# The unread elementwise result of a row maximum: one SBUF tile, or the PSUM bank it came from

## The chip, the cores and the metric

The kernel runs on one core of a Trainium2 chip. The metric is the device time of one execution in microseconds (us). The kernel before takes 852.42 us (median of 3 runs, 850.45 to 852.44).

The engines of the core have their own instruction queues, each worked in order, and wait for each other through semaphores: PE multiplies matrices and writes into PSUM, DVE (the vector engine) and ACT (the activation engine) read PSUM and SBUF, POOL works in SBUF, and SP issues the DMAs.

## The reference

One transformer block on 2048 tokens of width 512: layer norm, windowed causal attention with 32 heads of 16 columns and a window of 256 keys, output projection and residual, then a second layer norm and a gated MLP of hidden width 1376 with its residual.

```python
qkv = (x @ wqkv).reshape(B, S, 3, H, Dh)
scores = einsum("bhqd,bhkd->bhqk", q, k) * Dh ** -0.5
mask = (i - j >= 0) & (i - j < 256)
p = softmax(where(mask, scores, -1e9))
o = einsum("bhqk,bhkd->bhqd", p, v)
h = x + o @ wo
h2 = h + (sigmoid(ln(h) @ w_gate) * (ln(h) @ w_up)) @ w_down
```

The softmax needs, for each query and head, the maximum of the masked scores, or a number that serves as one. The change is in the place where that maximum is found.

## The kernel before, in words

Numbers are split into a high and a low float16 part, so a product of two matrices is three matmuls (`mm3`). The tokens go through attention in 8 blocks `b` of 256, and the heads in 8 groups `g` of 4. For a block and a group the stages are:

- `do_ln`, `do_qk`, `do_v`: layer norm, then the projections. PE writes into PSUM tiles of the ring `mm` (two banks), ACT and DVE copy them out in a high and a low part. SP moves queries and keys through DMAs into the tiles `SQ` and `SK`.
- `do_s`: the row maximum. For one head and one set of 64 query places, PE multiplies queries against 320 keys (at most two matmuls, L735, high parts alone) into a PSUM tile of the ring `s`, which has three banks. Then `row_max` lets DVE add the mask and take the maximum along the 320 columns in one instruction (L720). There are 512 of these, in the text called reductions, 448 of them 320 columns wide and the rest, of the first block, narrower.
- `do_m`: the maxima of a half of the heads are split, transposed by a DMA and written as extra rows into `SQ`, so that the next product comes out with the maximum subtracted.
- `do_st`: the scores once more, transposed and with both parts (`stp`, L789 to L800, ring of two banks). ACT takes the exponential (L765), POOL cuts the triangles at the window's ends off (L773, L778).
- `do_pv`, `do_o`, `do_wo`: probabilities times values (`pvp`, L826), transposed by DMA, divided by the row sums, multiplied by `wo` and added to `x`.

In the same stretch of time DVE, ACT and POOL also split and scale the weights of the MLP. The MLP (`do_ln2`, `do_pair`, `do_down`) follows the attention, with the last steps of attention in between.

An instruction of L720 has two results. The one that is read is the maximum, a column of the small tile `mq`; in the trace it appears as an instruction of its own, DVE_READ_ACCUMULATOR2_ANT, behind the CUSTOM_DVE_ANT_0 that does the work. The elementwise sum of scores and mask is also written, and nothing reads it: it goes to `junk`, a bfloat16 tile of 320 columns of which there is one (`bufs=1`).

The order of all instructions on every engine is written out: the table `ORDER` says which step of which piece comes next, and `Planner.run` follows it. The costs in the code have no part in it any more. What is not written by hand is the waits. The tile layer looks at what each instruction reads and writes, and gives it a wait on a semaphore wherever another instruction has to be done before. An instruction carries one wait itself; each further one stands as an EVENT_SEMAPHORE in front of it in the queue.

Of the kernel before, what the change touches and what calls it, by code (L numbers as in the profile page):

```python
# [28 lines left out]
BF16 = mybir.dt.bfloat16  # L29
# [6 lines left out]
P = 128  # L36
# [296 lines left out]
def tile_block(ctx, tc, x, wqkv, wo, wg, wu, wd, out):  # L333
    nc = tc.nc
    V, S, G, PE = nc.vector, nc.scalar, nc.gpsimd, nc.tensor
# [35 lines left out]
    def psum_tile(ring, shape, dt=F32):  # L371
        return psum.tile(shape, dt, name=ring + "p", tag=ring, bufs=RINGS[ring])
# [54 lines left out]
    swork = right.enter_context(tc.tile_pool(name="swork", bufs=2, side="right", reuse_waits="tile"))  # L427
# [16 lines left out]
    mask = swork.tile([P, 320], BF16, name="mask", bufs=1)  # L444
# [262 lines left out]
    def do_s(b, g, prio):  # L707

        p, hf = g // 2, g // 4
        needs = [("queries", b, p), ("filled", 0)] + [("keys", a, hf) for a in (b, b - 1) if a >= 0]  # L710
        left = 8

        def row_max(ps, c0, x, i, e, n):
            nonlocal left
            e, = yield {DVE_: (320 - c0) / 960 + 0.077}, [e]
            plan.free("s", n, e)
            junk = swork.tile([P, 320], BF16, name="junk", bufs=1)
            if (b, hf) not in mq:
                mq[b, hf] = swork.tile([P, 8, 4], F32, name="mq", bufs=4)
            V.tensor_tensor_reduce(out=junk[:, c0:], in0=ps[:, c0:], in1=mask[:, c0:], scale=1.0, scalar=-3.0e38,  # L720
                                   op0=ALU.add, op1=ALU.max, accum_out=mq[b, hf][:, x, i:i + 1])
            left -= 1
            if left == 0:
                plan.mark(("s", b, g), e)

        for jj in range(2):
            j = 2 * (g % 2) + jj
            for i in range(4):
                c0 = 0 if b else 256 - 64 * i
                e, n = yield {PE_: (320 - c0) / 2400 + 0.006}, needs, ["s"], 0.75  # L730
                ps = psum_tile("s", [P, 320])
                q = SQ[b % 2][0:96, 4 * p + j, i].rearrange("p u t -> p (u t)")
                for a, k0, k1, col in ((b - 1, 64 * i, 256, 0), (b, 0, 64 * i + 64, 256 - 64 * i)):
                    if a >= 0:
                        PE.matmul(ps[:, col:col + k1 - k0], q, SK[0:96, (2 * a + hf) % 5, 4 * (p % 2) + j, k0:k1], start=True, stop=True)  # L735
                plan.add(prio + (4 * jj + i) / 8, row_max(ps, c0, 4 * (p % 2) + j, i, e, n))
# [745 lines left out]
```

## Time and profile before

| what | before |
|---|---|
| median of 3 runs | 852.42 us |
| the profiled execution | 851.43 us |
| its span, first to last instruction | 849.6 us |
| mean granted TensorE clock | 0.97 of full speed |
| busy: PE, DVE, ACT, POOL | 90%, 85%, 52%, 33% of the span |
| first and last reduction (L720) | 45.4 and 482.7 us |

The profile has one row per group of instructions: line, engine, operation, out<-in with the sizes, how often, then the busy time and the mean of one, and behind a second bar the idle time of the engine just before them with what ended it. "DVE mq L720" as a releaser means that an engine waited until a reduction had written its maximum. "DVEq" is the sequencer of DVE, where the EVENT_SEMAPHORE instructions run. Matmuls are pipelined, and the records of successive ones overlap, so the busy share of PE is not the share of its peak.

### The profile page before, as it was taken

The page shows a single profiled execution, that of the slowest core. Times are in us where ns is not written, and L with a number is a line of the kernel's source. Part 1 is how long each engine was busy: PE and PEld are TensorE (multiplying, and loading weights), DVE is VectorE, ACT ScalarE, POOL GpSimd, SP SyncE. Part 2 cuts the span into 40 slices and gives each one's busy share as a digit, 9 for nine tenths or more (in the row PEclk, how much of TensorE's full clock was granted, in tenths as well). Part 3 has the DMA queues.
Part 4 walks back from the last instruction along what each step waited for, and adds up shares of the span by engine and source line. Part 5 has one row for each costly group of instructions (what it writes and reads, how often), then busy time and mean ns, then how long its engine had stood idle before and what let it go on. Part 6 is the DMA issues. An engine that isn't in the chain of part 4 may idle for free.

```text
span 849.6 us, 19062 instructions
## 1 busy us (share of the span) xinstructions
PE 765.7 (90%) x7014; PEld 509.9 (60%) x7014; DVE 725.9 (85%) x2052; ACT 438.2 (52%) x771; POOL 277.9 (33%) x342
## 2 busy tenths in 40 slices
PE   4788889999898899898999999658999999999997
PEld 3475557667666567566665555234756657567466
DVE  8988878888888889888987756999999888898983
ACT  5663656766568777767765766654221222112210
POOL 2632333424335354454445545655000000000000
PEclk9999988999999999999988999979999999999999
DMA  9585353374357459554965764974656458365536
GB/s 320 177 236 143 104 135 97 69 175 95 72 152 186 100 130 217 160 136 103 241 169 129 158 120 110 286 164 110 117 107 131 78 97 171 76 117 79 99 69 172
DMA packets 213326, 119.10 MB, mean 140 GB/s; under 512 B 176688, under 2 KB 185904, under 8 KB 213232
## 3 DMA queue, kind: packets, MB, share of 16 engines
q1 hardware_dynamic: 213232, 117.88, 59.1%
q8 instruction: 55, 0.90, 0.5%
q14 instruction: 39, 0.32, 0.1%
HBM read 43.65 MB, written 19.40 MB: 74 GB/s over the span
## 4 chain that ended last, share of the span: by engine, by line
PE 51%; DVE 32%; issue 7%; DMA 6%; ACT 1%; POOL 1%; DVEq 1%; SPq 0%; ACTq 0%; POOLq 0%
DVE junk L720 17%; PE sp L1131 12%; PE mmp L402 9%; PE mmp L1308 8%; PE pvp L826 6%; PE stp L1131 5%; PE sp L735 4%; PE pvp L1131 2%; PE stp L800 2%; PE stp L790 1%; DVE WD L951 1%; DMA x<-hl 1%; DVE sq L656 1%; PE mmp L1314 1%; DVE W L1021 1%
## 5 line engine op out<-in xcount | busy, mean ns | idle before, releaser
L720 DVE CUSTOM_DVE_ANT_0 junk<-sp,mask 128x320 bf16<-128x320 f32 (+4 forms) x512 | 239.5, 468 | 56.5 <-PE sp L735 9.3
L765 ACT ACTIVATE pa<-stp,kappa 128x512 f32<-128x512 f32 (+1 forms) x256 | 158.5, 645 | 81.5 <-PE stp L791 77.9
L735 PE MATMUL sp<-SK,SQ 96*128 96x256 f16 (+3 forms) x960 | 146.5, 237 | 37.3 <-DVE mq L720 29.1
L1131 PEld LDWEIGHTS <-x 128*128 128x128 f16 x1008 | 98.6, 98 | 105.9 <-issue 19.1
L1131 PE MATMUL sp<-W,x 128*128 128x512 f16 (+1 forms) x612 | 135.1, 361 | 14.2 <-DVE SQ L1154 10.5
L735 PEld LDWEIGHTS <-SQ 96*128 96x128 f16 x960 | 86.9, 99 | 86.9 <-issue 63.9
L402 PE MATMUL mmp<-xT,W 128*128 128x256 f16 x768 | 112.1, 276 | 4.9 <-DVE xT L357 2.2
L765 ACT ACTIVATE pb<-stp,kappa 128x512 f32<-128x512 f32 x128 | 85.6, 685 | 39.0 <-PE stp L800 38.1
L773 POOL TENSOR_SCALAR_AFFINE_SELECT pa<-pa 128x1024 f32<-128x1024 f32 x56 | 63.4, 1134 | 71.0 <-ACT pa L765 65.7
L402 PEld LDWEIGHTS <-W 128*128 128x128 f16 x768 | 70.3, 98 | 19.4 <-issue 5.0
L778 POOL TENSOR_SCALAR_AFFINE_SELECT pb<-pb 128x512 f32<-128x512 f32 x64 | 42.7, 667 | 71.4 <-ACT pb L765 64.2
L778 POOL TENSOR_SCALAR_AFFINE_SELECT pa<-pa 128x512 f32<-128x512 f32 x64 | 43.3, 677 | 65.3 <-ACT pa L765 65.3
L826 PE MATMUL pvp<-pa,VT 128*17 128x128 f32 (+1 forms) x1408 | 63.8, 312 | 0.6 <-DVE RH L838 0.6
L558 POOL TENSOR_TENSOR rs<-rs,nhalf 128x1 f32<-128x1 f32 x32 | 19.7, 619 | 131.5 <-DVE rs L555 131.2
L790 PE MATMUL stp<-SQ,SK 100*128 100x256 f16 x224 | 61.3, 278 | 0.0
L402 PE MATMUL mmp<-WO,oT 128*128 128x512 f16 x192 | 54.5, 405 | 5.5 <-DMA oT<-whl 5.3
L1131 PE MATMUL stp<-W,x 128*128 128x512 f16 (+1 forms) x264 | 58.2, 357 | 0.9 <-DVE SQ L359 0.6
L791 PE MATMUL stp<-SQ,SK 100*128 100x128 f16 x256 | 57.0, 223 | 0.2
L362 DVE TENSOR_TENSOR hr<-SQ,hr 128x512 f16<-128x512 f32 (+3 forms) x90 | 52.0, 588 | 2.4 <-ACT hr L355 1.6
L826 PEld LDWEIGHTS pvp<-pa,VT 128*17 128x17 f32 x1408 | 38.5, 99 | 24.7 <-issue 6.0
L800 PE MATMUL stp<-SQ,SK 100*128 100x256 f16 x256 | 50.5, 283 | 2.2 <-ACT pa L765 2.2
L1197 ACT ACTIVATE SQ<-sp,cg 128x512 f32<-128x512 f32 (+1 forms) x22 | 14.0, 638 | 73.2 <-PE sp L1131 73.2
(210 smaller groups left out, 1418.0 us busy)
## 6 DMA issues: line engine op xcount, KB each, us to landing
SQ<-sq SPq DMA_DIRECT2D x96, 128.0 KB
wr<-chunk SPq DMA_DIRECT2D x28, 256.0 KB
W<-wr SPq DMA_DIRECT2D x14, 512.0 KB
SK<-mem SPq DMA_DIRECT2D x16, 384.0 KB
chunk<-in_wd_dram SPq DMA_DIRECT2D x20, 256.0 KB
X<-in_x_dram SPq DMA_DIRECT2D x16, 256.0 KB
mem<-sk SPq DMA_DIRECT2D x8, 512.0 KB
out_dram<-X SPq DMA_DIRECT2D x16, 256.0 KB
```

The source lines that it names most:

```text
L402: PE.matmul(ps, a_of(a, k), b_of(b, k), start=(k == 0 and i == 0), stop=(k == n - 1 and i == 2))
L720: V.tensor_tensor_reduce(out=junk[:, c0:], in0=ps[:, c0:], in1=mask[:, c0:], scale=1.0, scalar=-3.0e38, op0=ALU.add, op1=ALU.max, accum_ou ...
L735: PE.matmul(ps[:, col:col + k1 - k0], q, SK[0:96, (2 * a + hf) % 5, 4 * (p % 2) + j, k0:k1], start=True, stop=True)
L765: S.activation(dst, a, AF.Exp, scale=kappa)
L773: G.affine_select(out=f, in_=f, pattern=[[0, 8], [-1, 128]], compare_op=ALU.is_gt, fill=0.0, base=0, channel_multiplier=1)
L778: G.affine_select(out=p, in_=p, pattern=[[0, 4], [1, 128]], compare_op=ALU.is_ge, fill=0.0, base=0, channel_multiplier=-1)
L790: PE.matmul(a[:, 128:384], ks(k0 + 1, g, j), qs(b, g, j, 0, 256), start=True, stop=True)
L791: PE.matmul(a[:, 384:512], ks(k0 + 3, g, j), qs(b, g, j, 128, 256), start=True, stop=True)
L800: PE.matmul(a[:, u, :], ks(k0 + 2, g, j + u), qs(b, g, j + u, 0, 256), start=True, stop=True)
L826: PE.matmul(ps[32 * j:32 * j + 17, u, q0:q1], VT[:, kt % 6, 8 * j + g, :], w[:, j, c:c + q1 - q0], start=first, stop=last, skip_group_chec ...
L1131: PE.matmul(ps, X2[p % 2][part][:, (a * COUNT[part] + at) * 2 + k, :], W[c][:, b, j, k, :], start=first and k == 0 and i == 0, stop=k == 1 ...
L1308: PE.matmul(ps, hT[p, c, r][:, a, half * kinds[c] + i, :], W["d"][2 * c + i][:, b, j, :], start=fresh and c == 0 and i == 0 and n == 0, st ...
```

## The change

The tile `junk` is gone. The elementwise sum is written back over the scores, into the same columns of the same PSUM tile that the instruction reads, in float32 in place of bfloat16. The mask, the maximum and its place in `mq` stay as they are, and the scores in that bank are read by nothing else afterwards: the next matmul of the ring `s` that gets the bank overwrites them.

```diff
@@ row_max, in do_s
             e, = yield {DVE_: (320 - c0) / 960 + 0.077}, [e]
             plan.free("s", n, e)
-            junk = swork.tile([P, 320], BF16, name="junk", bufs=1)
             if (b, hf) not in mq:
                 mq[b, hf] = swork.tile([P, 8, 4], F32, name="mq", bufs=4)
-            V.tensor_tensor_reduce(out=junk[:, c0:], in0=ps[:, c0:], in1=mask[:, c0:], scale=1.0, scalar=-3.0e38,
+            V.tensor_tensor_reduce(out=ps[:, c0:], in0=ps[:, c0:], in1=mask[:, c0:], scale=1.0, scalar=-3.0e38,
                                    op0=ALU.add, op1=ALU.max, accum_out=mq[b, hf][:, x, i:i + 1])
```

No instruction is added, removed or moved on any engine. What differs is the waits, and nearly all of that on DVE. On DVE, in the middle of the attention, the order before reads as follows; the first row is the end of one run of reductions, `mh0` takes the maxima of the run, and the last three rows begin the next run. The names in brackets are the semaphores that an instruction waits for, each with the engine that raises it.

```order
L720 ISA mq_1880 128x1
L369 TENSOR_REDUCE amu_624<-chunk_2090 128x1 [waits DMAHW2_49]
L742 TENSOR_SCALAR mh0_113<-mq_1880 128x32 [waits DMAHW4_49,DVE_49]
L743 SCALAR_TENSOR_TENSOR mh0_113<-mq_1880,mh0_113 128x32 [waits DVE_49]
L720 ISA junk_2462,mq_2463<-sp_2454,mask_109 128x320 [waits PE_49]
L720 ISA mq_2463 128x1
L720 ISA junk_2475,mq_2463<-sp_2465,mask_109 128x320 [waits DVE_49,PE_49]
```

The same place of DVE's queue after the change, one source line less:

```order
L719 ISA mq_1759 128x1
L369 TENSOR_REDUCE amu_622<-chunk_1954 128x1 [waits DMAHW2_49]
L741 TENSOR_SCALAR mh0_113<-mq_1759 128x32 [waits DMAHW4_49,DVE_49]
L742 SCALAR_TENSOR_TENSOR mh0_113<-mq_1759,mh0_113 128x32 [waits DVE_49]
L719 ISA sp_2294,mq_2302<-sp_2294,mask_109 128x320 [waits PE_49]
L719 ISA mq_2302 128x1
L719 ISA sp_2304,mq_2302<-sp_2304,mask_109 128x320 [waits PE_49]
```

Nothing moved; the last row waits for PE and DVE before, and for PE alone after. Of the 512 reductions 473 wait for DVE's own semaphore before, and 319 after. Before, for 363 of the 473 the value waited for is that of the reduction directly in front, the last writer of `junk`. After, in all but 12 of the 319, DVE has raised its semaphore twice or more since the value waited for, which is as a rule that of the reduction that had the same bank of the ring last. PE's waits, which let it reuse a bank of the ring `s` once the reduction has signalled, are the same.

## The prediction

> **What bounds the kernel now.** I read the page's shares first, then its chain of waits and its costliest groups.
>
> ```profile
> PE 765.7 (90%) x7014; PEld 509.9 (60%) x7014; DVE 725.9 (85%) x2052; ACT 438.2 (52%) x771; POOL 277.9 (33%) x342
> ```
> ```profile
> PE 51%; DVE 32%; issue 7%; DMA 6%; ACT 1%; POOL 1%; DVEq 1%; SPq 0%; ACTq 0%; POOLq 0%
> ```
> ```profile
> L720 DVE CUSTOM_DVE_ANT_0 junk<-sp,mask 128x320 bf16<-128x320 f32 (+4 forms) x512 | 239.5, 468 | 56.5 <-PE sp L735 9.3
> ```
>
> PE leads over the whole span, but the changed line runs from 45 to 483 us only, so that stretch decides. There I looked at the stage's window, the groups by shape, and the source line.
>
> ```profile
> 45.00:483.00 438.00, 396.62 (x4451) 278.40 (x4449) 376.29 (x1315) 294.72 (x513) 186.32 (x229) 0.96 0.58 140
> ...
> L720 DVE CUSTOM_DVE_ANT_0 junk<-sp,mask 128x320 bf16<-128x320 f32 x448 | 218.8, 488 | 50.3 <-PE sp L735 9.0 <-PE stp L791 1.0
> L720 DVE DVE_READ_ACCUMULATOR2_ANT mq<- 128x1 f32 x512 | 42.2, 83 | 0.0
> ...
> L720 DVEq EVENT_SEMAPHORE  x422: 21/21/21, 45.2 to 481.7; - x141
>   PE sp L735: 9.3, 17
>   PE stp L791: 1.0, 2
> ```
>
> The window row gives PE, weight loads, DVE, ACT, POOL, clock, DMA share and GB/s. DVE is busy for 376.3 of 438 us, idle for 62. Of that idle time 56.5 stands before L720, and PE ended only 9.3 + 1.0 of it. So 46.2 us of idle time before the reductions was ended by no other engine. The queue says why: 422 extra waits on this line. In the timeline of DVE they look like this:
>
> ```profile
> 253.52 0.48 DVE L720 CUSTOM_DVE_ANT_0 junk<-sp,mask 128x320 bf16<-128x320 f32 x1
> 253.93 0.08 DVE L720 DVE_READ_ACCUMULATOR2_ANT mq<- 128x1 f32 x1
> 254.16 0.49 DVE L720 CUSTOM_DVE_ANT_0 junk<-sp,mask 128x320 bf16<-128x320 f32 x1
> 254.57 0.08 DVE L720 DVE_READ_ACCUMULATOR2_ANT mq<- 128x1 f32 x1
> 254.80 0.49 DVE L720 CUSTOM_DVE_ANT_0 junk<-sp,mask 128x320 bf16<-128x320 f32 x1
> 255.22 0.08 DVE L720 DVE_READ_ACCUMULATOR2_ANT mq<- 128x1 f32 x1
> 255.44 0.49 DVE L720 CUSTOM_DVE_ANT_0 junk<-sp,mask 128x320 bf16<-128x320 f32 x1
> 255.86 0.08 DVE L720 DVE_READ_ACCUMULATOR2_ANT mq<- 128x1 f32 x1
> 255.86 0.69 DVE L838 SCALAR_TENSOR_TENSOR RH<-pvp,RH 128x512 f16<-128x512 f32 x1
> ```
>
> A reduction behind a reduction starts 0.64 us after it (254.16, 254.80, 255.44). L838, which does not wait for DVE, starts 0.42 us after the reduction in front of it (255.44 to 255.86), together with the reading of the maximum. The 0.22 us between is the wait for `junk`: the reduction in front must finish, signal, and be seen by DVE's sequencer. With DVE as its own blocker, DVE is taken for 376.3 + 46.2 = 422.5 of the stage's 438 us, 96%. It is the bound of the stage, and the chain of waits agrees:
>
> ```profile
> by line: DVE junk L720 32.3%; PE mmp L402 14.0%; issue 11.6%; PE pvp L826 9.3%; PE sp L735 7.1%; PE stp L800 2.6%; PE stp L790 2.1%; DVE sq L656 1.8%; DVE mq L720 1.6%; DMA RT<-RH 1.4%; PE stp L789 1.3%; PE stp L791 1.3%; DVE chunk L1021 1.
> ...
> 45.63 0.02 DVEq L720
> ...
> 151.47 0.49 DVE junk L720
> 151.97 0.02 DVE mq L720
> 151.99 0.03 issue
> 152.01 0.02 DVEq L720
> 152.03 0.08 issue
> 152.12 0.49 DVE junk L720
> ...
> 480.44 0.02 DVEq L720
> ```
>
> Reductions carry 32.3% of these 438 us, 141 us, which is 141/0.488 = 290 reductions' worth of 512. Each own wait on the chain is a piece "DVEq L720" between "issue" pieces; the first stands at 45.63, the last at 480.44, and there are 199 of them.
>
> **The change part by part.**
>
> *The own wait goes.* Such a wait shows as 0.145 us of idle time (254.57 + 0.08 to 254.80), so 46.2/0.145 gives some 320 of them; each frees 0.22 us of DVE, since the next reduction also overlaps the end of the one in front. DVE gains 320 x 0.22 = 70 us, and its need in the stage falls from 422 to 352 us. On the chain it is 199 x 0.22 = 44 us. That is the term of the sum, and a ceiling: what remains of this chain stays as long as it was.
>
> *The waits that stay.* The 319 reductions that still wait for DVE wait for a reduction about three places back, whose bank PE has already refilled; PE could only do that after its signal. So the wait is over when the instruction comes up, and its EVENT_SEMAPHORE (21 ns) runs while the reduction in front works. Price 0; if the sequencer were not ahead, the 21 ns on 290 chain reductions would be 6 us.
>
> *The write goes to PSUM in place of SBUF, 4 bytes for 2.* No row of DVE reads and writes one PSUM bank. From below: no gain beyond the wait, since the instruction streams the same 320 elements. Nearest rows for a price:
>
> ```profile
> L720 DVE CUSTOM_DVE_ANT_0 junk<-sp,mask 128x256 bf16<-128x256 f32 x16 | 6.8, 424 | 1.7
> ...
> L1201 DVE TENSOR_TENSOR SQ<-SQ 128x512 f32<-128x512 f32 x32 | 22.1, 693 | 3.2 <-ACT SQ L1197 2.5
> L359 DVE TENSOR_SCALAR SQ<-sp 128x512 f32<-128x512 f32 x11 | 7.6, 687 | 7.3 <-PE sp L1131 7.3
> ...
> L450 DVE MEMSET pvp<- x1: 485/485/485, 3.2 to 3.2; 128x512 f32 x1
> ...
> 187.82 1.30 PE mmp L402 x6
> ```
>
> 488 - 424 = 64 ns for 64 elements: about 1.0 ns per element, the rest fixed. Reading PSUM costs as much as reading SBUF (687 against 693 ns for 512 elements). The one instruction of DVE that writes PSUM, a memset, does 512 float32 in 485 ns, under 1 ns per element, so the write alone is no slower. Reading and writing one bank together: PE adds onto a bank at 1.30 us / (6 x 512) = 0.42 ns per column, more than twice as fast as DVE would read and write it. So I take 0. The other end is a bank that serves one access at a time, where read and write add up: 320 x 1.0 ns = 0.32 us per reduction, 290 x 0.32 = 93 us on the chain. I stay with 0, since PE's accumulation is the nearer row: it too reads and writes one bank.
>
> [...]
>
> *What is late next.* Three banks feed the reductions. PE needs its time too: in this stage its matmuls stream, at 0.42 ns per column, about 340 of 438 us, an estimate from these rows:
>
> ```profile
> L402 PE MATMUL mmp<-xT,W 128*128 128x256 f16 x768 | 112.1, 276 | 4.9 <-DVE xT L357 2.2 <-DVE sq L656 1.5 <-DVE W L534 1.1
> L402 PE MATMUL mmp<-WO,oT 128*128 128x512 f16 x192 | 54.5, 405 | 5.5 <-DMA oT<-whl 5.3 <-DVE sk L656 0.2
> L402 PE MATMUL mmp<-W,xT 128*128 128x512 f16 x192 | 51.4, 389 | 0.0
> ...
> 215.67 2.72 PE pvp L826 x64
> ```
>
> L402 has 768 x 256 + 384 x 512 = 393 thousand columns, some 80 thousand of them before 45 or after 483 us; the reductions have 448 x 320 and the first block's 10 thousand, 154 thousand; the second product has 3,072 columns for each of some 56 groups, 172 thousand. That is 640 thousand columns at 0.42 ns, 267 us, and about 27 pieces of L826 at 2.72 us, 74 us.
>
> Shortened by 44, the stage has 394 us, of which DVE needs 352 (89%) and PE 340 (86%). Two engines that work in order and hand each other three banks will wait for each other more than one engine at 96% and another at 78% do. The wait shown least now, that of L720 for PE (9.3 us), is what I expect to grow. I take 6 us of 44 back. ACT (295) and the DMAs (0.58) have room. After 483 us the order is unchanged and starts earlier; I count nothing there.
>
> **Sum.** The profiled execution took 851.4 us (span 849.6), 1.0 under the median of 852.4. 851.4 - 44 + 6 = 813.4; by the median 814. I forecast 814 us.
>
> **The rivals.**
>
> 1. *One bank, one access at a time* (slower). Place: every reduction; price 0.32 us. On the chain 93 - 44 = +49 us, 901; DVE alone would need 352 + 448 x 0.32 = 495 plus the narrow ones' 64 x 0.16 = 10, so over 500 us in place of 438, 852 + 67 or more. 900 to 925. It decides from 44/290 = 0.15 us per reduction on. For it: no row excludes it for DVE. Against: the accumulation at 0.42 ns. Chance 0.13.
>
> 2. *The gap is no wait but the engine's own flush* (no change). Then a reduction behind a reduction takes 0.64 us with or without a semaphore, and the time stays within 0.3% of 852 us (which is about what a measurement of this kernel can tell from no change). Against it: L838 at 255.86, 0.42 us after its reduction. For it: every pair of two reductions in the trace has the wait, so none shows what two do without. Chance 0.05. [...]
>
> 3. *PE takes the place of DVE or the write to PSUM costs a little* (faster by less). If the hand-over between PE and DVE lets PE stream for 82% of the stage and no more, the stage is 340/0.82 = 415 us and the gain 23. If a third of a reduction's fixed 0.17 us (488 - 320 x 1.0 ns) comes on top of each, the gain is 44 - 290 x 0.06 - 6 = 21, 831. For it: PE's matmuls of the reductions do wait now, 37.3 us of idle time (row below). Against it: the trace shows DVE at 96% and PE at 78%. Chance 0.17 for gains from 10 to 25, 827 to 842.
>
> The forecast itself, gains from 25 to 52 us, has 0.65: 800 to 827 us. That the change does not remove the wait at all is excluded by the instructions' waits.
>
> **How the numbers follow.** Faster 0.65 + 0.17 = 0.82, same 0.05, slower 0.13. The range reaches from 800 (the chain's 44 and some of PE's 29.1 us of waiting for a reduction, below) up to 842, where rival 3 ends; it leaves out rivals 1 and 2.
>
> ```profile
> L735 PE MATMUL sp<-SK,SQ 96*128 96x256 f16 (+3 forms) x960 | 146.5, 237 | 37.3 <-DVE mq L720 29.1
> ```
>
> **What would show it.** In the profile after: reductions of one run 0.42 us apart in the timeline; a CUSTOM of 320 still near 0.49 us (0.55 would be rival 3, 0.8 rival 1, 0.64 apart with 0.49 each rival 2); idle time before the line down from 56.5 to under 30 us, with PE as its releaser; fewer than 422 extra waits, some 320; the last reduction at about 445 in place of 482.7 us; PE's waiting for a reduction below 29.1 us; and the time after that point unchanged, 367 us. The prediction fails if the duration grows by over 0.15 us, or if most of the freed time turns into DVE waiting for PE.

## The result and the profile after

The changed kernel takes 794.08 us (median of 4 runs, 789.39 to 796.94) against 852.18 before. The ratio is 0.932, with a 95% interval of 0.927 to 0.936. The forecast was 814 us and the range 800 to 842: the direction was right, the gain of 58 us half as large again as forecast, and the time lies under the range.

The profiled execution took 793.8 us, its span is 792.1. The first reduction starts at 45.6 us and the last at 424.5, so the stretch of the reductions fell from 437.4 to 378.9 us, by 58.5. What follows it took 366.9 us before and takes 367.6 now. The whole gain lies in the stage that the prediction looked at.

The page's busy shares and its row of the changed line after the change, and then, from the view of that source line, its rows and the two lists of waits (first what ended DVE's idle time before it, then who waited for it):

```profile
PE 737.8 (93%) x7014; PEld 502.7 (63%) x7014; DVE 712.5 (90%) x2052; ACT 434.7 (55%) x771; POOL 277.0 (35%) x342
...
L719 DVE CUSTOM_DVE_ANT_0 sp<-sp,mask 128x320 f32<-128x320 f32 (+4 forms) x512 | 227.1, 494 | 8.7 <-PE sp L734 6.7
...
L719 DVE DVE_READ_ACCUMULATOR2_ANT mq<- x512: 82/141/146, 45.8 to 424.9; 128x1 f32 x171
L719 DVEq EVENT_SEMAPHORE  x318: 21/21/21, 45.5 to 423.7; - x159
  PE sp L734: 6.7, 18
...
  PE sp L734: 6.4, 17
```

The idle time before the reductions fell from 56.5 to 8.7 us, and 6.7 of what is left is ended by PE. PE's own waiting for a reduction fell from 29.1 to 6.4 us. The extra waits in DVE's queue are 318, about what the order of the changed program has (319 reductions wait for DVE), and cost nothing visible. One row is not as expected: reading the maximum takes 141 ns (median), not 83. In the timeline of DVE:

```profile
250.11 0.49 DVE L719 CUSTOM_DVE_ANT_0 sp<-sp,mask 128x320 f32<-128x320 f32 x1
250.52 0.14 DVE L719 DVE_READ_ACCUMULATOR2_ANT mq<- 128x1 f32 x1
250.52 0.53 DVE L719 CUSTOM_DVE_ANT_0 sp<-sp,mask 128x320 f32<-128x320 f32 x1
250.97 0.14 DVE L719 DVE_READ_ACCUMULATOR2_ANT mq<- 128x1 f32 x1
250.97 0.53 DVE L719 CUSTOM_DVE_ANT_0 sp<-sp,mask 128x320 f32<-128x320 f32 x1
251.42 0.13 DVE L719 DVE_READ_ACCUMULATOR2_ANT mq<- 128x1 f32 x1
251.42 0.53 DVE L719 CUSTOM_DVE_ANT_0 sp<-sp,mask 128x320 f32<-128x320 f32 x1
```

A reduction now starts together with the reading of the maximum in front of it, as only other instructions did before. Two of them stand 0.45 us apart (250.52, 250.97, 251.42), 0.42 was forecast, 0.64 it was. Only the first of a run, which starts beside no reading, is followed after 0.41 us (250.11, 250.52). This speaks directly against the rival by which an engine's own flush makes the gap. The same two instructions are 0.19 us closer without the wait.

The stage's window (PE, weight loads, DVE, ACT, POOL, clock, DMA share, GB/s) reads:

```profile
45.63:424.49 378.86, 365.89 (x4447) 269.14 (x4445) 363.54 (x1312) 290.52 (x512) 184.65 (x228) 1.00 0.69 162
```

DVE works for 363.5 of 378.9 us, 96%: the share that it was taken before, when its own waits are counted in. DVE's need, busy time and own waits together, fell from 422 to 363.5 us, by about 58.6, and the stage by 58.5. That is the first hint to what was wrong: the stage shrank with DVE's need, and not with the chain of waits. PE's busy share rose beside it, from 90% to 97% (365.9 of 378.9 us; its records overlap).

### The profile page after: what moved, and what is told of

The parts are those of the page before. It is cut to its first block, busy times and chain, and to the rows that moved or that the text cites. A ratio compares the mean times of both kernels' runs of the same rounds, so it can differ in the third digit from the quotient of the medians.

```text
span 792.1 us, 18959 instructions
## 1 busy us (share of the span) xinstructions
PE 737.8 (93%) x7014; PEld 502.7 (63%) x7014; DVE 712.5 (90%) x2052; ACT 434.7 (55%) x771; POOL 277.0 (35%) x342
## 5 line engine op out<-in xcount | busy, mean ns | idle before, releaser
L719 DVE CUSTOM_DVE_ANT_0 sp<-sp,mask 128x320 f32<-128x320 f32 (+4 forms) x512 | 227.1, 494 | 8.7 <-PE sp L734 6.7
L734 PE MATMUL sp<-SK,SQ 96*128 96x256 f16 (+3 forms) x960 | 136.3, 231 | 10.4 <-DVE mq L719 6.4
L402 PE MATMUL mmp<-xT,W 128*128 128x256 f16 x768 | 113.7, 281 | 4.2 <-DVE xT L357 2.2
L734 PEld LDWEIGHTS <-SQ 96*128 96x128 f16 x960 | 83.0, 97 | 46.2 <-issue 22.2
L719 DVE DVE_READ_ACCUMULATOR2_ANT mq<- 128x1 f32 x512 | 70.7, 138 | 0.2
L789 PE MATMUL stp<-SQ,SK 100*128 100x256 f16 x224 | 59.9, 272 | 0.0
L1130 PE MATMUL stp<-W,x 128*128 128x512 f16 (+1 forms) x264 | 58.6, 358 | 0.8 <-DVE SQ L359 0.7
L402 PE MATMUL mmp<-WO,oT 128*128 128x512 f16 x192 | 51.0, 384 | 4.8 <-DMA oT<-whl 4.7
```

Of the source, the lines that this page charges most:

```text
L402: PE.matmul(ps, a_of(a, k), b_of(b, k), start=(k == 0 and i == 0), stop=(k == n - 1 and i == 2))
L719: V.tensor_tensor_reduce(out=ps[:, c0:], in0=ps[:, c0:], in1=mask[:, c0:], scale=1.0, scalar=-3.0e38, op0=ALU.add, op1=ALU.max, accum_out= ...
L789: PE.matmul(a[:, 128:384], ks(k0 + 1, g, j), qs(b, g, j, 0, 256), start=True, stop=True)
L1130: PE.matmul(ps, X2[p % 2][part][:, (a * COUNT[part] + at) * 2 + k, :], W[c][:, b, j, k, :], start=first and k == 0 and i == 0, stop=k == 1 ...
```

## The experiments

Two theories stood against each other. **A**: DVE's whole load sets the length of the stage, so every own wait that goes counts, wherever the chain of waits was drawn. **B**: only the waits on the chain count, 44 to 48 us, and the rest of the gain came from elsewhere, from PE's clock for instance. Counted in the trace of before by the starts of the instructions, 363 of the 512 reductions stand directly behind another and wait for it. At 0.227 us for the 322 with an extra EVENT_SEMAPHORE in front and 0.118 for the other 41 that makes 78 us. Not all of it is the own wait's: 15 of them start more than 0.26 us after the reading in front, so something else came later there. The other 348 add up to 74 us (the prediction had taken some 320 and 70 us).

**The wait without the destination.** Two tiles in SBUF in place of one.

```diff
-            junk = swork.tile([P, 320], BF16, name="junk", bufs=1)
+            junk = swork.tile([P, 320], BF16, name="junk", bufs=2)
-                mq[b, hf] = swork.tile([P, 8, 4], F32, name="mq", bufs=4)
+                mq[b, hf] = swork.tile([P, 8, 4], F32, name="mq", bufs=2)
-        mt = swork.tile([P, 1, P], F16, name="mt")
+        mt = swork.tile([P, 1, P], F16, name="mt", bufs=1)
```

> The kernel before with two SBUF tiles for the unread result in place of one; room for the second comes from two tiles that lose spare buffers (mq 4 to 2, mt 2 to 1). Each reduction then waits for the one two places back, which is done. So the own wait goes as in the change, and the destination stays SBUF. Theory A (DVE's whole load sets the length of the attention stage, wherever the chain of waits was drawn): two reductions stand 0.416 us apart, 0.033 less than the 0.449 of the changed kernel, so the time falls below the changed kernel's by about 448 x 0.033 = 15 us, to 779. Theory B (only the waits on the chain of waits count, 44 to 48 us, and the rest of the 58 us came from PE's clock, which was granted at 0.66 to 0.86 in parts of the stage before and at 1.00 after): no further gain, 790 to 797.

Measured: 788.16 us, ratio 0.926 (0.922 to 0.930). The spacing of two reductions is 0.411 us (median), the reading of the maximum 0.083 us again:

```profile
252.66 0.48 DVE L720 CUSTOM_DVE_ANT_0 junk<-sp,mask 128x320 bf16<-128x320 f32 x1
253.07 0.08 DVE L720 DVE_READ_ACCUMULATOR2_ANT mq<- 128x1 f32 x1
253.07 0.48 DVE L720 CUSTOM_DVE_ANT_0 junk<-sp,mask 128x320 bf16<-128x320 f32 x1
253.48 0.08 DVE L720 DVE_READ_ACCUMULATOR2_ANT mq<- 128x1 f32 x1
253.48 0.68 DVE L362 TENSOR_TENSOR whl<-OS,whl 128x512 f16<-128x512 f32 x1
```

So the gain is that of the wait, and PSUM has no part in it but a price. The time falls between the two theories' numbers (779, and 790 to 797); other runs have to tell them apart.

**The destination without the wait's going.** PSUM as in the change, and an own wait by another path: all reductions write their maximum into one column. The kernel leaves out the subtraction of the maximum, since `mq` is filled with zeros.

```diff
+                G.memset(mq[b, hf], 0.0)
+            one = swork.tile([P, 1], F32, name="one", bufs=1)
-                                   op0=ALU.add, op1=ALU.max, accum_out=mq[b, hf][:, x, i:i + 1])
+                                   op0=ALU.add, op1=ALU.max, accum_out=one)
```

> The changed kernel with its own wait put back: all reductions write their maximum into one shared column, so each waits for the one in front; the tile of maxima is filled with zeros, that is, the subtraction of the maximum is left out of the computation. What remains against the kernel before is the destination in PSUM alone. In the changed kernel the reading of the maximum takes 0.141 in place of 0.083 us. Theory A: with the wait behind it the 0.058 us come on top of every spacing, 0.70 in place of 0.643 us, and 363 x 0.058 = 21 us are lost, about 870 to 874. Theory B: 223 of the waits on the chain, 13 us, 865. If writing PSUM costs nothing when nothing overlaps it: 852.

Measured: 878.90 us, ratio 1.031 (1.027 to 1.036), slower than before. The spacing is 0.701 us, here 301.08 to 301.79:

```profile
301.08 0.50 DVE L721 CUSTOM_DVE_ANT_0 sp<-sp,mask 128x320 f32<-128x320 f32 x1
301.50 0.14 DVE L721 DVE_READ_ACCUMULATOR2_ANT one<- 128x1 f32 x1
301.79 0.50 DVE L721 CUSTOM_DVE_ANT_0 sp<-sp,mask 128x320 f32<-128x320 f32 x1
```

The reduction is as long as before to within 0.01 us; the reading of the maximum carries the 0.058 us, and behind a wait all of it is paid (a spacing of 0.70 us in place of 0.64). The loss of 26 us is some 5 more than 363 x 0.058 = 21; where the rest comes from was not measured.

**What it is about the destination.** Sixteen reductions more, ahead of everything else:

```diff
+    bankA, bankB, place = psum_tile("s", [P, 320]), psum_tile("st", [P, 512]), chunks.tile([P, 512], F32, name="chunk")
+    found = keep.tile([P, 16], F32, name="found")
+    V.memset(bankA, 0.0)
+    V.memset(mask, 0.0)
+    for n in range(16):
+        to = (place.bitcast(BF16)[:, :320], place[:, :320], bankB[:, :320], bankA)[n // 4]
+        V.tensor_tensor_reduce(out=to, in0=bankA, in1=mask, scale=1.0, scalar=-3.0e38,
+                               op0=ALU.add, op1=ALU.max, accum_out=found[:, n:n + 1])
```

> The kernel before with 16 reductions of 320 columns more, ahead of everything else, on a bank of zeros: four write a bfloat16 place in SBUF, four a float32 place in SBUF, four another bank of PSUM, four the bank they read. The price of the destination is read from the rows. If PSUM as a destination is the cause of the longer reading of the maximum: 0.083, 0.083, 0.141, 0.141 us. If it is the one bank: 0.083, 0.083, 0.083, 0.141. If it is the 4 bytes: 0.083, 0.141, 0.141, 0.141. The reduction itself about 0.49 to 0.50 us in all.

Measured, one pair of rows for each destination in the order of the list (`chunk` is the place in SBUF, `stp` the other bank, `sp` the bank that is read):

```profile
5.22 0.49 DVE L458 CUSTOM_DVE_ANT_0 chunk<-sp,mask 128x320 bf16<-128x320 f32 x1
5.64 0.08 DVE L458 DVE_READ_ACCUMULATOR2_ANT found<- 128x1 f32 x1
...
7.36 0.49 DVE L458 CUSTOM_DVE_ANT_0 chunk<-sp,mask 128x320 f32<-128x320 f32 x1
7.77 0.08 DVE L458 DVE_READ_ACCUMULATOR2_ANT found<- 128x1 f32 x1
...
9.43 0.50 DVE L458 CUSTOM_DVE_ANT_0 stp<-sp,mask 128x320 f32<-128x320 f32 x1
9.84 0.14 DVE L458 DVE_READ_ACCUMULATOR2_ANT found<- 128x1 f32 x1
...
12.34 0.50 DVE L458 CUSTOM_DVE_ANT_0 sp<-sp,mask 128x320 f32<-128x320 f32 x1
12.75 0.14 DVE L458 DVE_READ_ACCUMULATOR2_ANT found<- 128x1 f32 x1
```

Neither the 4 bytes nor the one bank matters. Either bank of PSUM as the destination makes the reading of the maximum behind it 0.06 us longer (0.14 against 0.08).

**Only the waits beside the chain.** The reductions alternate between two tiles in SBUF only where a wait is to go; where the tile stays the same, the own wait stays. `FREE` holds the numbers of the reductions, here the 140 whose own wait was no piece of the listed chain of before (`mq` and `mt` as in the first experiment).

```diff
+    FREE = frozenset([...])
+    J = [swork.tile([P, 320], BF16, name=f"junk{i}", bufs=1) for i in range(2)]
+    seen = [0, 0]
-            junk = swork.tile([P, 320], BF16, name="junk", bufs=1)
+            seen[1] ^= seen[0] in FREE
+            seen[0] += 1
+            junk = J[seen[1]]
```

> SBUF destination, two tiles, with the tiles alternated only where the own wait did not lie on the chain of waits of the kernel before: 140 of the 363 waits go, the 223 on the chain stay. The freed DVE time is 123 x 0.227 + 17 x 0.118 = 30 us. Theory A: the stage shortens by most of it, about the same share as in the change (58 of 75 to 80 us freed), so 22 to 25 us, 828. Theory B: nothing on the chain is shorter, 849 to 852.

Measured: 830.59 us, ratio 0.975 (0.971 to 0.980), 22 us faster than before. Theory B is refuted in its main point: waits that the chain does not show are worth 22 us, of 30 that were counted as freed, or 26 without those where something else came later. PE's clock can have given only a part of it: its mean in the stage was 0.97 against 0.96 before, so 0.03 x 419 = 12.6 us were lost against 0.04 x 437 = 17.5 (at a clock of 0.50, as granted before from 127 to 132 us, that is some 25 us of the stage against 35), which is 5 us of lost work less, an estimate.

**Only the waits on the chain.** The same edit with the other 223 numbers.

> The complement: the 223 waits on the chain of waits go, the 140 beside it stay. Freed DVE time 199 x 0.227 + 24 x 0.118 = 48 us. Theory A: a gain of 35 to 40 us, 812 to 817, and the gains of this and of the kernel with the other 140 freed add up to that of the kernel with all freed. Theory B: the whole 44 to 48 us, 804 to 808, as much as with all waits freed.

Measured: 803.63 us, ratio 0.944 (0.939 to 0.948), 49 us. Freed were 48, so these return in full. That is just under theory B's number; theory A's even share, 812 to 817, is missed. The two gains add up to 71 us, 7 to 8 more than freeing all at once, where theory A had them add up. So a wait on the chain is worth its whole length and one beside it most of its length.

**Which of the 140.** Theory B could still be saved: the listed chain has holes. The chain's list of before has a single transfer for the time from 290.19 to 294.46 us:

```profile
290.16 0.03 PE stp L791
290.19 4.26 DMA SK<-mem
294.46 0.03 issue
294.49 0.08 DVE mq L720
```

In that time DVE does this, and up to 294.46 us never stops but for itself:

```profile
291.50 0.49 DVE L720 CUSTOM_DVE_ANT_0 junk<-sp,mask 128x320 bf16<-128x320 f32 x1
291.91 0.08 DVE L720 DVE_READ_ACCUMULATOR2_ANT mq<- 128x1 f32 x1
292.14 0.49 DVE L720 CUSTOM_DVE_ANT_0 junk<-sp,mask 128x320 bf16<-128x320 f32 x1
292.56 0.08 DVE L720 DVE_READ_ACCUMULATOR2_ANT mq<- 128x1 f32 x1
292.79 0.49 DVE L720 CUSTOM_DVE_ANT_0 junk<-sp,mask 128x320 bf16<-128x320 f32 x1
```

So the 140 were parted: 38 that fall under a piece named issue, DMA or ACT, and 102 that fall under a piece of PE. The edit is the same, with other numbers in `FREE`.

> As the kernel that frees the waits beside the chain, but only 38 of those 140: the ones that fall in time under a piece of the chain named issue, DMA or ACT (at 290.19 to 294.46 us the chain names one DMA, while DVE runs a row of reductions with own waits). Freed DVE time about 38 x 0.22 = 8 us. Theory B2 (the listed chain has holes, and under them the own waits were on the true path): the whole 7 to 8 us, 844 to 846. Theory A (DVE's load counts, wherever): the same share as for all 140, 22 of 30, so 5 to 6 us, 847.

Measured: 844.34 us, ratio 0.991 (0.989 to 0.993): 7.5 us, nearly the whole of the 8 freed and theory B2's number: under a hole of the list a wait counts like one on the chain.

> The other 102 of the 140 are freed, those that fall in time under a piece of the chain that names PE. Freed DVE time about 102 x 0.21 = 22 us. Theory B2: next to nothing, 849 to 852, since PE's pieces stay as long as they were. Theory A: 22/30 of it, 15 to 16 us, 837. Theory C (PE waits less, so the granted clock is at half for fewer us, 34 in the stage before and 24 with all 140 freed): some of what B2 denies, 3 to 5 us, 848.

Measured: 839.13 us, ratio 0.985 (0.983 to 0.986): 12.7 us of the 22 counted as freed (19 without those where something else came later), less than theory A's 15 to 16 and far from B2's nothing. If PE's pieces of the chain had bound the stage, this would be nothing but what the clock gives. The clock was granted at 0.97 in the stage against 0.96 before, which is 0.01 x 425 = 4 us at most, an estimate; so it cannot have made all of the 12.7.

**PE's own room.** The last matmul of each reduction's scores is issued twice.

```diff
                     if a >= 0:
                         PE.matmul(ps[:, col:col + k1 - k0], q, SK[...], start=True, stop=True)
+                PE.matmul(ps[:, col:col + k1 - k0], q, SK[...], start=True, stop=True)
```

> The kernel before with the last matmul of each reduction's scores issued twice (the second overwrites the first with the same values): PE gets 512 matmuls more, 160 columns on average, 512 x 0.067 = 34 us of streaming in the stage, DVE nothing. Theory A: PE had room, so the time grows by less than 8 us. Theory B2: what lies on PE's pieces of the chain grows, the reductions' matmuls there are 31 of 150 us, so about 34 x 31/150 = 7 us and more if PE's room is used up. Theory C: with PE busier the clock is at half for less than the 34 us of the stage before, under 20, and the time may even fall.

Measured: 850.52 us, ratio 0.999 (0.997 to 1.001): no change. The stage's window of this kernel:

```profile
45.25:482.02 436.77, 412.38 (x4958) 305.53 (x4957) 376.81 (x1313) 294.83 (x513) 185.44 (x229) 1.00 0.59 141
```

PE runs 512 matmuls more and its clock is granted at 1.00 in the stage, where it was 0.96. The lost clock was 438 x 0.04 = 17 us at most, so at least 34 - 17 = 17 us of added streaming are swallowed: PE had room, as theory A says. How much the risen clock gave and how much the added work took cannot be parted in this run, so theory C, by which the clock pays, is not excluded for the other 17.

**The change and the two tiles side by side, and PE's room then.** The changed kernel again; the two tiles again; and the two tiles with the matmul issued twice.

> The changed kernel itself, beside the one with two SBUF tiles on the same chip, to tell the two apart. The destination in PSUM makes a spacing of two reductions 0.449 in place of 0.411 to 0.416 us: DVE loses 448 x 0.033 = 15 us. If DVE alone sets the stage, 12 to 15 us slower than the two tiles; if PE has become nearly as late, 4 to 7 us, as the first runs (794.1 against 788.2) say.

> The kernel with two SBUF tiles again, on the same chip as the changed kernel: 786 to 790 us if the first runs hold, and its interval below that of the changed kernel.

> Two SBUF tiles, and the last matmul of each reduction's scores issued twice as before: 34 us more streaming for PE. On the kernel before this changed the time by 0.1%, since PE waited anyway and its clock rose. If PE is now late as often as DVE (in the two-tile kernel 13.8 us of the idle time before the reductions are ended by PE, 9.3 before): most of the 34 us come through, 808 to 820. If DVE is still the only bound: under 8 us, 788 to 796.

Measured: the change 792.96 us, ratio 0.932 (0.928 to 0.935); two tiles 787.98, ratio 0.926 (0.923 to 0.929); two tiles and more work for PE 808.15, ratio 0.950 (0.947 to 0.953). The two tiles are 5 us faster than the change here and 6 in the first runs. The two intervals overlap at their ends, so the order of the two rests on both pairs of runs. The stage's windows of the change and of the two tiles:

```profile
45.81:426.76 380.95, 366.26 (x4447) 269.13 (x4445) 364.00 (x1314) 290.62 (x513) 183.93 (x228) 1.00 0.69 161
```
```profile
46.36:419.54 373.18, 362.54 (x4447) 269.18 (x4445) 350.78 (x1314) 288.41 (x512) 184.78 (x227) 1.00 0.71 164
```

DVE is busy 13 us less with the two tiles (350.8 against 364.0), and the reductions wait 7 us longer for PE (13.6 against 7.0): about 6 us are left, as measured. The row of the reductions shows the waiting, first for the two tiles, then with PE's added work:

```profile
L720 DVE CUSTOM_DVE_ANT_0 junk<-sp,mask 128x320 bf16<-128x320 f32 (+4 forms) x512 | 214.4, 464 | 15.3 <-PE sp L735 13.6
```
```profile
L720 DVE CUSTOM_DVE_ANT_0 junk<-sp,mask 128x320 bf16<-128x320 f32 (+4 forms) x512 | 220.1, 466 | 29.5 <-PE sp L736 25.6
```

The same 34 us of PE that cost nothing before cost 20 here, and DVE's waiting for PE doubles. With the own wait gone and SBUF as the destination, PE and DVE bound the stage together.

## Why the prediction was right or wrong

- *What bounds the stage*: right in the main. DVE with its own waits was taken for 96% of it, and added work for PE cost no time, though PE's clock rose with it.
- *The own wait and its price*: right. The 0.22 us per wait is 0.227 for most, and the waits of the trace that decided a start add up to 74 us where 70 stood; with two SBUF tiles DVE's need fell from 422 to 351 us, 352 was forecast.
- *"On the chain it is 199 x 0.22 = 44 us. That is the term of the sum, and a ceiling"*: this is the step that failed. The ceiling took the listed chain for the longest path. It is a list of inferred releasers, and it left DVE for PE, DMA and issue at places where DVE did not stop but for itself. The 140 waits that it left out were worth 22 us by themselves. The count was short as well: besides the 199 waits with a piece "DVEq L720" the chain holds 24 that the instruction carries itself, and all 223 were worth 49 us by measurement. The DVE term of the prediction, which stood beside it, was the one to go by: DVE's need fell by 58.6 us, with the price of the destination in it, and the stage by 58.5.
- *The waits that stay, price 0*: right. 318 extra waits remain, and the idle time before the line is 8.7 us in all.
- *The write to PSUM, price 0*: wrong by 0.033 to 0.038 us per spacing (0.449 against 0.411 to 0.416), 13 us of DVE's busy time and 5 to 6 us of time. A reduction that stands alone does not get slower, as argued (0.50 us); the reading of its maximum does, by 0.058 us, and a reduction that starts together with such a reading is recorded at 0.53 us. The rows for a price were those of the streaming instruction; none was for what follows it. The 687 and 693 ns compared there are two different instructions; the same one, TENSOR_TENSOR, takes 682 ns with a source in PSUM (L1152) and 693 without, so that reading stands for these instructions.
- *What is late next, 6 us back*: wrong for the change. DVE's need and the stage fell by the same 58.5 us, and L720's waiting for PE fell from 9.3 to 6.7 us. It grows only when the destination's price is gone as well, to 13.6; there DVE's need fell by 71 us and the stage by 63 to 64.
- *After 483 us*: right, 366.9 and 367.6 us.
- *The rivals*: one access at a time was excluded by 0.53 us per reduction and by the 0.50 of another bank; the flush by the spacing of 0.45; a small price per reduction was real and was outweighed. A hand-over that lets PE stream for 82% of the stage and no more did not come: even the prediction's 340 us of streaming are 90% of 378.9.

The runs give the sum in four terms: 49 us for the waits on the chain, 22 for those beside it, 7 back because the two gains overlap (all at once gave 64.6 with two SBUF tiles), and 6 back for the destination. That is 58. The term of 44 was thus too small by 5, and 22 stood at nothing. Why the two gains overlap by 7 us was not measured by itself.

## What to carry to other kernels

Here the engine that was 96% taken, its own waits counted in, set the pace of its stage in the main, whatever the listed chain of waits showed beside it. In such a stage, count what is freed on that engine first, and use the chain to find the waits, not to cap their sum: what lay on it returned in full here (49 us where 48 were freed), what lay beside it to more than half (22 of 30). A scratch tile that nothing reads still orders its writers: with one buffer 363 of the 512 reductions here waited for the whole of the one in front, its signal included, and stood as a rule 0.53 to 0.65 us behind it; with a second buffer the spacing was 0.411 us. Where there is no room in SBUF for one, the operand's own PSUM bank may do: here it served nearly as well, and the second tile, at the price of spare buffers elsewhere, is 5 to 6 us faster than the change (787.98 against 792.96 us side by side).

## What the runs showed of the hardware that was not expected

- An own wait cost more here where it stood as an extra instruction. In the chain of before, a reduction that waits for DVE alone starts 0.53 us after the one in front (152.12 to 152.65), and one that waits for PE as well 0.64 to 0.65 us (151.47 to 152.12). Of the 363, the 322 with an EVENT_SEMAPHORE in front are of the second kind and the 41 without of the first:

```profile
151.47 0.49 DVE junk L720
...
152.12 0.49 DVE junk L720
152.61 0.02 DVE mq L720
152.63 0.02 issue
152.65 0.49 DVE junk L720
```

- A PSUM destination lengthened the reading of the accumulator behind it from 0.083 to 0.141 us, in both banks that were tried.
- PE's granted clock in the stage was 0.96 before, 1.00 in the changed kernel and 1.00 when PE got 34 us of useless work. What lowers it is not shown. In the kernel before it was low from 110 to 130 us, where PE was busy for 7.6 and 8.7 of 10 us, but not from 160 to 170, where it was busy for 8.6 (columns as above):

```profile
110.00:120.00 10.00, 7.59 (x62) 5.09 (x54) 7.85 (x33) 6.07 (x15) 3.65 (x6) 0.79 0.43 99
120.00:130.00 10.00, 8.70 (x77) 5.54 (x77) 7.47 (x31) 5.33 (x13) 3.02 (x6) 0.67 0.35 118
160.00:170.00 10.00, 8.63 (x75) 5.91 (x75) 8.20 (x33) 7.44 (x13) 5.09 (x7) 1.00 0.50 102
```

The clock fell there without a long pause of PE: from 100 to 170 us no gap between two matmuls is longer than 0.65 us. The runs of before reach from 846.9 us at a mean clock of 0.976 to 854.6 at 0.968, the shorter ones as a rule with the higher clock. So some of the 58 us may be the clock's, at most the 17 us that it lost in the stage before (0.04 x 438, an estimate); how much was not measured apart.
